# A causal convolution by Fourier transform beside linear attention: a planner's order replaced by tables, with transform pieces of 64 channels

## The chip, the cores and the metric
The kernel runs on one core of a Trainium2 chip. The time is device microseconds of one execution, from launch to end. Five engines work from queues of their own: TensorE (PE, with its weight loads shown as PEld), VectorE (DVE), ScalarE (ACT), GpSimd (POOL) and SyncE (SP), which here issues every DMA. An engine takes its instructions strictly in order, so one that waits holds up all that stand behind it on that engine.

## The reference
Two independent blocks of 2048 positions and 576 channels, bf16, their outputs side by side.

```python
# A: short convolution of k over 4 taps, product with v, long causal convolution by FFT, gate by q
k_shift = sum(k_pad[:, t:t+S, :] * shift_k[:, ks-1-t] for t in range(4))
kv = k_shift * v
y = irfft(rfft(kv padded to 2S) * rfft(ssm_k padded to 2S))[:S] + kv * ssm_D
a = q * y
# B: linear attention with 32 heads of 18 channels
qh, kh, vh = heads of (x @ wqkv);  phi(t) = where(t > 0, t + 1, exp(t)) + 1e-6
o = (phi(qh) @ (phi(kh)' @ vh)) / (phi(qh) . sum(phi(kh)) + 1e-6)
b = o @ wo
out = concatenate([a, b], axis=-1)
```

## The kernel before
**Block A.** The position is split as n = 16a + b, with a on the 128 partitions. Channels go in three chunks (`cc`) of 192. `conv_piece` (L507) does the short convolution on VectorE for one chunk and one half of the sixteen b (`bh`): two tap products of 3072 elements (L518), two sums (L523, L526), a product with v (L529), in place in v. The taps lie in `Wj`, the same row on all partitions: `Wall` is loaded by a DMA that broadcasts 576 KB, and one ScalarE copy of 2304 elements (L493) puts it in order. `h_piece` turns the long filter's rows (`hs`, six pieces of 96 channels) into columns by TensorE transposes.

The transform has two stages. `s1` (L570) multiplies by the tables `Gsb`: for real and imaginary part and for each half of b, eight matmuls of 192 columns into a four-bank PSUM tile, half a bank apart, and one ScalarE copy of 1536 elements (L585) into `Ch` (filter, "h") or `Cu` (signal, "u"). `s2` (L594) takes pieces of `PCH` = 48 channels: a VectorE transpose in 32x32 blocks (L600), 16 small matmuls of 384 columns into a four-bank tile (L612), and two copies of 768 elements by ScalarE or VectorE (L395, L397, the helper `copy`). For the filter, two DMAs (`X`) swap neighbouring partitions into a second tile. `inv` (L632) multiplies the signal's piece by the filter's two tiles (L636, L639), 32 small matmuls (L647) go into a four-bank tile, and two copies put 24 channels each into `V`. There are 12 pieces for h and 12 for u; six pieces make one half of V (288 channels).

`inv2` (L659) ends block A for each half: V goes to a DRAM scratch `v_scr` in rows of 576 bytes, comes back in four loads of `Vt` (rows of 2304 bytes, with the transform index on the partitions), eight matmuls with `Esb` make four positions b (L678), VectorE multiplies by q (L683), and the result is stored.

**Block B.** `kproj` (L693, 16 of them) and `qproj` (L715, 10) project transposed x (`xT`, four groups loaded by transposing DMAs, L445 and L448), ScalarE takes the exponential, VectorE makes phi into `pk` and `pqT`. `b_G` (L755, five) multiplies x by pk, 32 matmuls each; from that come `kvb`, `M` (which holds wo) and the denominators `rden` (a VectorE reciprocal). `b_bc` (L865) spreads rden over the heads' channels in a four-bank tile and VectorE normalizes pqT (L877, ten products of 1024 elements). `b_out` (L883) makes 16 output blocks of 128 positions: ten matmuls of 288 columns (L890), one copy, one store.

**Order.** Each step is an operation of a `Prog` with its engine (or a choice of ScalarE and VectorE), a cost, and what it reads and writes. `Prog.schedule` (L107) issues them in the order of a list schedule: longest remaining path plus a hand-set `BIAS` by group, with `LORDER` for the first loads and limits on live buffers in `LIMIT`. It also places each buffer in SBUF and each tile in PSUM. The order of the result is the order in which instructions go to the engines.

Of the kernel before, what the change touches and what calls it, by code (L numbers as in the profile page):

```python
# [23 lines left out]
PCH = 48  # L24
# [3 lines left out]
class Buf:  # L28
    def __init__(self, name, shape, dt=BF, space="sb", side=0, banks=0, pre=False):
        self.pre = pre  # L30
        self.name, self.shape, self.dt, self.space, self.side, self.banks = name, list(shape), dt, space, side, banks
# [5 lines left out]
        self.left = 0  # L37
        self.pos = None
        self.keys = {}
        self.t = None  # L40
# [6 lines left out]
LAT = 0.12  # L47
SBUF_LO = 16512
SBUF_HI = 229344
DMA_LAT = 2.0  # L50
INF = 1e18


class Prog:
# [9 lines left out]
    def op(self, engs, fn, rd=(), wr=(), name="", bias=0.0, tx=0.0, after=(), use=()):  # L64
# [3 lines left out]
        o.fn, o.name, o.bias, o.tx = fn, name, bias, tx  # L68
# [38 lines left out]
    def schedule(self):  # L107
        ops = self.ops
        n = len(ops)
        succ = [[] for _ in range(n)]  # L110
        nd = [0] * n
        for o in ops:
            for d in o.deps:
                succ[d].append(o.id)
            nd[o.id] = len(o.deps)
        cp = [0.0] * n
        for o in reversed(ops):
            own = min(o.engs.values()) + (o.tx + DMA_LAT if "SP" in o.engs else LAT)
            cp[o.id] = own + max([cp[s] for s in succ[o.id]] + [0.0])
        for o in ops:  # L120
            o.prio = cp[o.id] + (BIAS[o.bias[0]] + o.bias[1] if isinstance(o.bias, tuple) else o.bias)
        engs = ("PE", "ACT", "DVE", "POOL", "SP")
        free = dict.fromkeys(engs, 0.0)
        ready = [0.0] * n
        cand = {e: [] for e in engs}
        for b in self.bufs:
            b.left, b.pos, b.last = b.users, None, 0.0
        for o in ops:
            if nd[o.id] == 0:
                for e in o.engs:  # L130
                    cand[e].append(o)
        bank_free = [0.0] * 8
        live = []
        dma_free = 0.0
        order = []

        def place_ps(b, t):
            best = None
            step = b.banks
            for p in range(0, 8 - b.banks + 1, step):  # L140
                f = max([t] + bank_free[p:p + b.banks])
                if f < INF / 2 and (best is None or f < best[0] - 1e-9):
                    best = (f, p)
            return best

        def place_sb(b, t):
            times = sorted(set([t] + [x[2] for x in live if t < x[2] < INF / 2]))
            lim = LIMIT.get(b.name, 99)
            for tt in times:
                if sum(1 for x in live if x[2] > tt and x[3].name == b.name) >= lim:  # L150
                    continue
                busy = sorted((x[0], x[1]) for x in live if x[2] > tt)
                if b.side == 0:
                    at = SBUF_LO
                    for s, e in busy:
                        if s - at >= b.nbytes:
                            return tt, at
                        at = max(at, e)
                    if SBUF_HI - at >= b.nbytes:
                        return tt, at  # L160
                else:
                    at = SBUF_HI // 32 * 32
                    for s, e in reversed(busy):
                        if at - e >= b.nbytes:
                            return tt, at - b.nbytes
                        at = min(at, s)
                    if at - SBUF_LO >= b.nbytes:
                        return tt, at - b.nbytes
            return None

        def try_place(o, t):
            got = []
            added = []
            ok = True
            saved = None
            for b in o.bufs:
                if b.pos is not None or b.space == "dram":
                    continue
                r = place_ps(b, t) if b.space == "ps" else place_sb(b, t)
                if r is None:  # L180
                    ok = False
                    break
                t = max(t, r[0])
                got.append((b, r[1]))
                if b.space == "sb":
                    added.append([r[1], r[1] + b.nbytes, INF, b])
                    live.append(added[-1])
            for x in added:
                live.remove(x)
            return (t, got) if ok else None  # L190

        for b in self.bufs:
            if b.pre:
                b.pos = place_sb(b, 0.0)[1]
                live.append([b.pos, b.pos + b.nbytes, INF, b])
# [776 lines left out]
```

## Time and profile before

| | before |
|---|---|
| median of 3 runs | 215.75 us (215.52 to 216.03) |
| profiled execution | 215.91 us, span 214.1 us |
| TensorE busy | 164.7 us (77%), 1800 matmuls |
| VectorE busy | 154.9 us (72%), 161 instructions |
| ScalarE busy | 120.8 us (56%), 141 instructions |
| mean granted clock of TensorE | 0.857 of full |
| DMA | 40.09 MB, mean 187 GB/s |

The span runs from the first to the last instruction. Busy time of TensorE counts its pipelined matmuls by modelled ends, so a busy TensorE is not one at its peak. The granted clock is a share of 2.4 GHz.

### The profile page before, as it was taken

How to read it: one execution, taken by the hardware profiler on the slowest of the kernel's cores; microseconds unless marked ns; L12 is line 12 of the kernel's file. 1: busy time of each engine (PE TensorE's matmuls, PEld its weight loads, DVE VectorE, ACT ScalarE, POOL GpSimd, SP SyncE). 2: the span in 40 equal slices, each digit the busy share in tenths (PEclk: the TensorE clock that was granted, in tenths of full speed). 3: DMA queues.
4: the chain of work that ended last, by engine and by line, in shares of the span. 5: the costliest groups of instructions: out<-in, count | busy, mean ns of one | idle time of the engine just before them, and what ended most of it. 6: DMA issues, size and time to landing. Idle time of an engine off the chain costs nothing.

```text
span 214.1 us, 4250 instructions
## 1 busy us (share of the span) xinstructions
PE 164.7 (77%) x1800; PEld 109.6 (51%) x1800; DVE 154.9 (72%) x161; ACT 120.8 (56%) x141; POOL 6.7 (3%) x17
## 2 busy tenths in 40 slices
PE   0660917997898997975899998787577775899993
PEld 0340616655656654751677686255122641576772
DVE  0029999999999899959773073999999799804220
ACT  2071325645989589788846435998986400043442
POOL 7100000000000000100000000000000000000000
PEclk9996785699998799997599999955855895599999
DMA  6899999999340002772790000141199999968543
GB/s 172 199 378 271 362 339 270 215 233 351 97 147 5 2 0 108 237 245 77 300 282 11 0 3 0 53 175 73 41 309 315 298 321 324 354 230 245 187 135 125
DMA packets 39965, 40.09 MB, mean 187 GB/s; under 512 B 11850, under 2 KB 34635, under 8 KB 39178
## 3 DMA queue, kind: packets, MB, share of 16 engines
q1 hardware_dynamic: 39946, 39.82, 61.1%
q8 instruction: 14, 0.23, 0.4%
q14 instruction: 5, 0.04, 0.0%
HBM read 23.04 MB, written 9.44 MB: 152 GB/s over the span
## 4 chain that ended last, share of the span: by engine, by line
PE 40%; DVE 29%; DMA 11%; ACT 10%; issue 7%; SPq 2%; POOL 0%; DVEq 0%; ACTq 0%
PE ps_all L890 10%; PE ps_all L761 9%; DMA Vt<-v_scr 5%; PE ps_all L702 5%; DMA hs<-in_A_ssm_k_dram 5%; DVE m L518 4%; PE ps_all L724 4%; PE ps_all L580 4%; DVE pk L710 3%; DVE ct L600 3%; DVE m L523 3%; ACT Cu L585 3%; PE ps_all L678 2%; DVE sph L636 2%; DVE X L639 2%
## 5 line engine op out<-in xcount | busy, mean ns | idle before, releaser
L702 PE MATMUL ps_all<-wk,xT 128*128 128x288 bf16 x160 | 24.9, 316 | 16.2 <-DMA xT<-in_B_x_dram 14.0
L702 PEld LDWEIGHTS <-xT 128*128 128x128 bf16 x160 | 16.6, 107 | 23.6 <-DMA xT<-in_B_x_dram 14.8
L395 ACT ACTIVATE ob<-ps_all 128x576 bf16<-128x576 f32 x16 | 10.4, 651 | 29.2 <-PE ps_all L890 29.2
L580 PEld LDWEIGHTS <-Gsb 128*128 128x128 bf16 x192 | 20.6, 115 | 8.6 <-issue 5.5
L724 PE MATMUL ps_all<-xT,wq 128*126 128x512 bf16 (+1 forms) x100 | 24.1, 391 | 0.6 <-DVE pqT L731 0.6
L710 DVE SCALAR_TENSOR_TENSOR pk<-ek,ps_all 128x576 bf16<-128x576 bf16 x16 | 11.8, 747 | 16.4 <-ACT ek L707 16.4
L890 PE MATMUL ps_all<-M,pqT 126*128 126x288 bf16 (+1 forms) x160 | 22.0, 299 | 0.5 <-DVE q L683 0.5
L612 PE MATMUL ps_all<-ct,cst 32*32 32x384 bf16 x384 | 15.4, 383 | 8.2 <-DVE ct L600 2.8
L683 DVE TENSOR_TENSOR q<-ps_all,q 128x1152 bf16<-128x1152 f32 x8 | 10.6, 1354 | 15.1 <-PE ps_all L678 15.0
L761 PE MATMUL ps_all<-pk,x_sb 128*128 128x288 bf16 (+1 forms) x160 | 20.6, 286 | 0.6 <-ACT Cu L585 0.4
L518 DVE TENSOR_TENSOR m<-kh,Wj 128x3072 bf16<-128x3072 bf16 x12 | 20.6, 1751 | 0.1
L585 ACT ACTIVATE Ch<-ps_all 128x1536 bf16<-128x1536 f32 x12 | 18.0, 1503 | 2.9 <-PE ps_all L580 2.9
L585 ACT ACTIVATE Cu<-ps_all 128x1536 bf16<-128x1536 f32 x12 | 17.5, 1510 | 3.5 <-PE ps_all L580 3.1
L890 PEld LDWEIGHTS <-pqT 126*128 126x128 bf16 (+1 forms) x160 | 16.3, 102 | 5.9 <-issue 0.7
L707 ACT ACTIVATE ek<-ps_all,neg 128x576 bf16<-128x576 f32 x16 | 11.5, 736 | 13.0 <-PE ps_all L702 11.5
L761 PEld LDWEIGHTS <-x_sb 128*128 128x128 bf16 x160 | 15.5, 98 | 4.8 <-issue 1.0
L724 PEld LDWEIGHTS <-wq 128*126 128x126 bf16 (+1 forms) x100 | 13.2, 137 | 8.7 <-issue 1.9
L580 PE MATMUL ps_all<-v,Gsb 128*128 128x192 bf16 x96 | 14.3, 325 | 2.2 <-ACT Cu L585 1.2
L728 ACT ACTIVATE eq<-ps_all,neg 126x1024 bf16<-126x1024 f32 (+1 forms) x10 | 11.1, 1113 | 7.6 <-PE ps_all L724 7.5
L612 PEld LDWEIGHTS <-cst 32*32 32x32 bf16 x384 | 5.3, 90 | 18.8 <-issue 12.3
L600 DVE STREAM_TRANSPOSE ct<-Ch 128x768 f32<-128x768 f32 x12 | 11.3, 963 | 4.5 <-ACT Ch L585 4.2
L395 ACT ACTIVATE sph<-ps_all 128x768 bf16<-128x768 f32 x18 | 13.8, 824 | 1.0 <-PE ps_all L612 0.9
(63 smaller groups left out, 236.1 us busy)
## 6 DMA issues: line engine op xcount, KB each, us to landing
X<-sph SPq DMA_DIRECT2D x24, 192.0 KB, 2.2
v_scr<-V SPq DMA_DIRECT2D x2, 2304.0 KB, 12.2
Vt<-v_scr SPq DMA_DIRECT2D x8, 576.0 KB, 7.3
v<-in_A_v_dram SPq DMA_DIRECT2D x2, 1152.0 KB, 10.0
hs<-in_A_ssm_k_dram SPq DMA_DIRECT2D x6, 384.0 KB, 11.0
x_sb<-in_B_x_dram SPq DMA_DIRECT2D x1, 2304.0 KB, 10.9
q<-in_A_q_dram SPq DMA_DIRECT2D x2, 1152.0 KB, 6.6
out_dram<-q SPq DMA_DIRECT2D x8, 288.0 KB, 4.8
```

The costliest lines, as they stand in the source:

```text
L395: nc.scalar.activation(out=o, in_=i, func=ACTF.Copy)
L518: nc.vector.tensor_tensor(out=m.t[:, i:i + 2], in0=i0, in1=i1, op=ALU.mult)
L580: nc.tensor.matmul(ps.t[:, j // 2, 256 * (j % 2):256 * (j % 2) + CC], lhsT=Gsb.t[:, b, ri, :], rhs=src, start=True, stop=True)
L585: nc.scalar.activation(out=C.t[:, :, rb:rb + 8, :].rearrange("p w r t -> p r w t"), in_=ps.t.rearrange("p b (h c) -> p (b h) c", h=2)[:, : ...
L600: nc.vector.transpose(out=ct.t[:].rearrange("p w r t -> p (w r t)").bitcast(FP32), in_=C.t[:, nw * pi:nw * pi + nw].rearrange("p w r t -> ...
L612: nc.tensor.matmul(o, lhsT=W2()[32 * kh:32 * kh + 32, :], rhs=ctf[32 * kh:32 * kh + 32, 384 * j:384 * j + 384], start=True, stop=True)
L702: nc.tensor.matmul(ps.t[:, hh, 0:HALF], lhsT=xT.t[:, t, 128 * rr:128 * rr + 128], rhs=wk.t[:, t, HALF * hh:HALF * hh + HALF], start=(t == ...
L707: P.op(("ACT", _act(576) + 0.09), lambda e: nc.scalar.activation(out=eb.t[:], in_=ps.t[:, :, 0:HALF], func=ACTF.Exp, bias=neg1.t[:]), rd=[ ...
L710: P.op(("DVE", _dve(576)), lambda e: nc.vector.scalar_tensor_tensor(out=pk.t[:, r, 0:D].rearrange("p (h c) -> p h c", h=2), in0=eb.t[:], s ...
L724: nc.tensor.matmul(ps.t[0:hn, j, :], lhsT=wq.t[:, t, h0:h0 + hn], rhs=xT.t[:, t, :], start=(t == 0), stop=(t == 4))
L761: nc.tensor.matmul(ps.t[:, hh, 0:n], lhsT=x_sb.t[:, r, FT[t]:FT[t] + 128], rhs=pk.t[:, r, HALF * hh:HALF * hh + n], start=(r == 0), stop=( ...
L890: nc.tensor.matmul(ps.t[:, hh, 0:HALF], lhsT=pqT.t[0:hn, c, 128 * r:128 * r + 128], rhs=M.t[0:hn, c, HALF * hh:HALF * hh + HALF], start=(c ...
```

## The change
The planner is gone. Two tables stand in its place: `PLAN`, one word for each of the 573 operations in issue order with its engine, and `PLACES`, the place of each buffer. With it:

- `PCH` is 64, so there are 9 pieces for h and 9 for u. A piece's second stage and its inverse each run as two steps in two-bank PSUM tiles, with matmuls of 512 columns and copies of 1024 elements. The products with the filter are of 2048 elements, and the `X` swaps are issued in the signal's part.
- The first stage packs its eight blocks of 192 columns without gaps into three banks; a block that straddles a bank is two matmuls. Its copy may be on either engine.
- V's halves are 320 and 256 channels (five and four pieces). V is written to DRAM in one run per partition; it is read back in 32 loads of 32 partitions (every fourth one), in rows of 640 or 512 bytes. The last stage works in two-bank tiles: eight steps of two positions for the first half, four of four for the second.
- The taps come as one row of 4.6 KB; matmuls of a row of ones with it spread the row over the partitions, and two ScalarE copies of 1152 elements make `Wj`.
- The first 192 columns of `kh0` and of its three earlier rows are loaded apart from the rest.
- The normalization runs in ten steps of two banks, so the second half's positions can go first.

In the table, the queue of TensorE begins with the filter's transposes and its first stage, then the first k blocks; the five G blocks stand together with the last filter pieces and the first chunk of u; seven normalizations, M and output blocks 9, 13 and 14 stand ahead of the last piece of V; ten output blocks stand between it and the first i2 step of V's second half. SP's queue begins with cst, hs, khh, Drow, hs, srow, Gsb, kh0 (192 columns), khh, then xT 0, wk, xT 1, v0, kh1, wq, v1, three hs, the rest of kh0, and the transposed loads of groups 2 and 3.

```diff
-PCH = 48
+PCH = 64
+VN = (320, 256)
+VP = (0, 5)
...
-    order = P.schedule()
+    order = _issue(P)
...
+def _issue(P):
+    names = dict(P="PE", A="ACT", D="DVE", G="POOL", S="SP")
+    order = []
+    for w in PLAN.split():
+        o = P.ops[int(w[1:])]
+        o.eng = names[w[0]]
+        order.append(o)
+    places = [int(w) for w in PLACES.split()]
+    for b, p in zip([b for b in P.bufs if b.space != "dram"], places, strict=True):
+        b.pos = p
+    return order
...
-    load("Wall", Wall, lambda e: dma(Wall.t[:].rearrange("p d j -> p (d j)"),
-                                     A_shift_k.rearrange("d j -> (d j)").partition_broadcast(128)), 589824,
+    load("srow", srow, lambda e: dma(srow.t[:], A_shift_k.rearrange("(o d) j -> o d j", o=1)), 4608,
+    for hh in range(2):
+        wps = psb(4, "wps")
+        def wmm(e, hh=hh, wps=wps):
+            for j in range(4):
+                nc.tensor.matmul(wps.t[:, j, 0:HALF], lhsT=ones.t[0:1, :],
+                                 rhs=srow.t[0:1, HALF * hh:HALF * hh + HALF, j], start=True, stop=True)
...
-                ps = psb(4, "s1ps")
+                ps = psb(3, "s1ps")
...
+                        for bank, lo, hi in banks(CC * j, CC * j + CC):
+                            nc.tensor.matmul(ps.t[:, bank, lo - 512 * bank:hi - 512 * bank], lhsT=Gsb.t[:, b, ri, :],
+                                             rhs=src[:, lo - CC * j:hi - CC * j], start=True, stop=True)
...
+        for kp in range(2):
+            ps = psb(2, "s2ps")
+            def mm(e, kp=kp, ps=ps):
+                for j in range(4):
+                    for kk in range(2):
+                        kh = 2 * kp + kk
+                        nc.tensor.matmul(
+                            ps.t[32 * j:32 * j + 32, kk, :].rearrange("p (k w t) -> p w k t", w=8, t=2),
+                            lhsT=W2()[32 * kh:32 * kh + 32, :], rhs=ct.t[32 * kh:32 * kh + 32, 8 * j:8 * j + 8],
+                            start=True, stop=True)
...
+            P.op(either(1024), lambda e, kp=kp, ps=ps: copy(e, sp.t[:, 2 * kp:2 * kp + 2, :], ps.t),
...
-        w_ = load("Vw", None, lambda e: dma(ap(vd, 0, [[HALF, 128], [128 * HALF, 32], [1, HALF]]), V[hf].t[:]),
+        load("Vw", None, lambda e: dma(vd, V[hf].t[:].rearrange("p k c -> p (k c)")), 8192 * n, rd=[V[hf]], wr=[dtok],
...
+                vt = SB("Vt", [128, 8, n])
+                for kh in range(4):
+                    load("Vr", vt, lambda e, b4=bg * nb, vt=vt, kh=kh: dma(
+                        vt.t[kh:128:4], ap(vd, (32 * kh + 2 * b4) * 32 * n, [[n, 32], [32 * n, 8], [1, n]])),
```

## Rows read from the trace of the kernel before

**Rows 1.** Busy time by stretch: from:to us, length, busy us (count) of each engine, clock, DMA share, GB/s.
```profile
0.00:14.90 14.90, 6.77 (x40) 4.34 (x40) 0.01 (x1) 4.32 (x4) 4.56 (x13) 1.00 0.83 237
14.90:92.30 77.40, 60.06 (x482) 42.04 (x483) 76.22 (x77) 49.46 (x52) 2.12 (x4) 0.87 0.66 196
92.30:139.30 47.00, 39.24 (x585) 26.97 (x585) 28.05 (x32) 31.38 (x41) 0.00 (x0) 0.93 0.29 100
139.30:166.80 27.50, 20.72 (x423) 10.03 (x423) 26.52 (x31) 23.23 (x29) 0.00 (x0) 0.58 0.61 186
166.80:185.50 18.70, 13.18 (x85) 7.56 (x84) 17.51 (x19) 1.96 (x3) 0.00 (x0) 0.77 1.09 319
185.50:214.10 28.60, 24.71 (x189) 18.69 (x187) 6.63 (x6) 10.42 (x16) 0.00 (x0) 0.96 0.61 197
sum 214.10, PE 164.68 PEld 109.63 DVE 154.94 ACT 120.76 POOL 6.68; mean PE 27.45 PEld 18.27 DVE 25.82 ACT 20.13 POOL 1.11
```

**Rows 2.** Chain of waits, in order of time: start us, us, what.
```profile
107.14 4.11 PE ps_all L761 x32
...
171.55 11.08 DMA Vt<-v_scr
...
210.76 0.65 ACT ob L395
```

**Rows 3.** Groups of VectorE instructions: total us, mean ns of one, idle before.
```profile
L636 DVE TENSOR_TENSOR sph<-spu,sph 128x1536 bf16<-128x1536 bf16 x12 | 11.3, 944 | 0.0
L600 DVE STREAM_TRANSPOSE ct<-Ch 128x768 f32<-128x768 f32 x12 | 11.3, 963 | 4.5 <-ACT Ch L585 4.2 <-PE ps_all L612 0.2
L683 DVE TENSOR_TENSOR q<-ps_all,q 128x1152 bf16<-128x1152 f32 x8 | 10.6, 1354 | 15.1 <-PE ps_all L678 15.0
L877 DVE SCALAR_TENSOR_TENSOR pqT<-pqT,ps_all 126x1024 bf16<-126x1024 bf16 x8 | 9.3, 1212 | 0.0
L397 DVE CAST V<-ps_all 128x768 bf16<-128x768 f32 x8 | 7.4, 951 | 0.6 <-PE ps_all L647 0.5
L397 DVE CAST spu<-ps_all 128x768 bf16<-128x768 f32 x7 | 6.5, 937 | 1.6 <-PE ps_all L612 1.6
L397 DVE CAST sph<-ps_all 128x768 bf16<-128x768 f32 x6 | 5.4, 935 | 0.0
L397 DVE CAST M<-ps_all 126x576 bf16<-126x576 f32 x1 | 0.7, 746 | 0.0
```

**Rows 4.** Groups of ScalarE copies from PSUM.
```profile
L585 ACT ACTIVATE Cu<-ps_all 128x1536 bf16<-128x1536 f32 x12 | 17.5, 1510 | 3.5 <-PE ps_all L580 3.1 <-DVE sph L397 0.5
L395 ACT ACTIVATE spu<-ps_all 128x768 bf16<-128x768 f32 x17 | 13.3, 823 | 0.9 <-PE ps_all L612 0.9
```

**Rows 5.** SP's queue at the start, in order of time: start us, us, instruction.
```profile
9.09 9.36 SPq L445 DMA_TRANSPOSE xT<-in_B_x_dram  x1
...
23.25 12.81 SPq L445 DMA_TRANSPOSE xT<-in_B_x_dram  x1
```

**Rows 6.** Busy time in three stretches; the last column is DMA in GB/s.
```profile
0.00:30.00 30.00, 13.36 (x80) 8.61 (x80) 15.00 (x13) 9.06 (x10) 5.07 (x14) 0.89 0.92 290
158.00:163.80 5.80, 4.11 (x98) 1.19 (x98) 5.80 (x7) 5.13 (x8) 0.00 (x0) 0.50 1.13 302
171.50:177.30 5.80, 4.15 (x33) 2.52 (x31) 5.71 (x6) 0.30 (x1) 0.00 (x0) 1.00 1.13 316
```

**Rows 7.** SP's queue from the first write of V on.
```profile
153.61 0.40 SPq L382 DMA_DIRECT2D v_scr<-V  x1
...
163.87 1.87 SPq L382 DMA_DIRECT2D Vt<-v_scr  x3
167.01 0.38 SPq L382 DMA_DIRECT2D v_scr<-V  x1
...
181.31 4.01 SPq L382 DMA_DIRECT2D Vt<-v_scr  x3
```

**Rows 8.** Output blocks on TensorE, in order of time.
```profile
193.75 5.09 PE L890 MATMUL ps_all<-M,pqT 126*128 126x288 bf16 x40 [0.47 <-DVE q L683]
```

More of the change, by code (lines that the diff above doesn't have):

```diff
@@ L269 @@
-WIN = 0.05
+def _issue(P):
[8 more added lines that the diff above has]
+        b.pos = p
+    assert sorted(o.id for o in order) == list(range(len(P.ops)))
+    return order
 def _tables():
@@ L331, in _tables, with banks @@
     return G.astype(bf), E.astype(bf), C.astype(bf)
+def banks(lo, hi):
+    got = []
+    while lo < hi:
+        e = min(hi, lo // 512 * 512 + 512)
+        got.append((lo // 512, lo, e))
+        lo = e
+    return got
 def _pe(*ns):
@@ L338, in _act, with _dma @@
 def _act(n):
-    return 0.19 + n * 0.000833
+    return 0.17 + n * 0.000868
 def _dve(n, rate=1):
-    return 0.065 + n * 0.00104 / rate
-def _dma(nb):
-    return nb / 330000.0
+    return 0.145 + n * 0.001045 / rate
+def _dma(nb, row=4096):
+    return nb / (16.0 * row / (8.0 + row * 0.0412) * 1000.0)
 @with_exitstack
@@ L462, in f2 @@
             dma(wx.t[64:128, 4, :], wqkv[512:576, c0:c0 + D])
-        load("wqk" + key, wx, f1, 589824, wr=[(wx, "m")])
+        load("wqk" + key, wx, f1, 589824, wr=[(wx, "m")], row=1152)
         load("wqkt" + key, wx, f2, 73728, wr=[(wx, "t")])
@@ new lines, in s2 @@
+        for kp in range(2):
[8 more added lines that the diff above has]
+                            start=True, stop=True)
+            aft = [seq[x] for x in (nm, ("h", g)) if x in seq] if kp == 0 else []
+            last = P.op(("PE", T8), mm, rd=[ct, cst], wr=[ps], use=[sp], name="s2" + nm, bias=bias, cnt=8, after=aft)
+            P.op(either(1024), lambda e, kp=kp, ps=ps: copy(e, sp.t[:, 2 * kp:2 * kp + 2, :], ps.t),
+                 rd=[ps], wr=[(sp, kp)], name="s2ev" + nm, bias=bias)
@@ new lines, in s2 @@
+        seq[nm] = last
+        seq[(nm, g)] = last
+        if nm == "h":
+            TX[g] = sp
+        return g, sp
+    V = [SB("V%d" % i, [128, 32, VN[i]], side=1) for i in range(2)]
+    def inv(g, su, bias):
+        tx = TX[g]
+        hf = int(g >= VP[1])
+        c0 = PCH * (g - VP[hf])
+        xb = SB("X", [128, 4, 512])
+        load("X", xb, lambda e: dma(xb.t[0:128:2], tx.t[1:128:2]), 262144, rd=[tx], wr=[(xb, 0)], bias=bias, row=4096)
+        load("X", xb, lambda e: dma(xb.t[1:128:2], tx.t[0:128:2]), 262144, rd=[tx], wr=[(xb, 1)], bias=bias, row=4096)
+        P.op(("DVE", _dve(2048, 2)),
@@ new lines, in inv, with mm, ev @@
+        for jp in range(2):
+            ps = psb(2, "i1ps")
+            def mm(e, jp=jp, ps=ps):
+                for wi, (w, src) in enumerate(((W31, tx), (W32, xb))):
+                    for kh in range(4):
+                        for jj in range(2):
+                            j = 2 * jp + jj
+                            nc.tensor.matmul(ps.t[32 * kh:32 * kh + 32, jj, :],
+                                             lhsT=w()[32 * j:32 * j + 32, :],
+                                             rhs=src.t[32 * j:32 * j + 32, kh, :],
+                                             start=(wi == 0), stop=(wi == 1))
+            P.op(("PE", 2 * T8), mm, rd=[tx, xb, cst], wr=[ps], use=[V[hf]], name="i1", bias=bias, cnt=16)
+            def ev(e, jp=jp, ps=ps):
+                o0 = c0 + 32 * jp
+                copy(e, V[hf].t[:, :, o0:o0 + 32].rearrange("p k (j c) -> p j k c", c=16),
+                     ps.t.rearrange("p j (k c) -> p j k c", c=16))
+            P.op(either(1024), ev, rd=[ps], wr=[(V[hf], (g, jp))], name="i1ev", bias=bias)
```

470 lines of the change are left out of this document (144 added, 326 removed), and 12 rows, old and new, of the table PLACES.

## The prediction
> **What bounds the kernel now.** I read the busy time by stretch first [rows 1]. VectorE is the fullest engine with 154.9 of 214.1 us, and its idle time has three places. In the first 14.9 us it does nothing. From 14.9 to 92.3 us it is busy 76.2 of 77.4 us, so there its own work is the limit. From 92.3 to 139.3 us it is busy for only 28.05 of 47 us; there the chain of waits runs through TensorE blocks of 32 matmuls of 4.11 us each (the product x'·pk, five of them) and through what queues behind them [rows 2]. From 139.3 to 166.8 us, the stage of products and inverse transforms, VectorE is full again, 26.52 of 27.5 us. At 166.8 us the last piece of V has left PSUM. What follows takes 47.3 us, more than a fifth of the time, and holds no transform of the first stages at all: V goes to DRAM and comes back, VectorE normalizes all of pqT (17.5 of 18.7 us busy), the chain waits 11.08 us for Vt [rows 2], and only then TensorE starts the 16 output blocks, which fill the last 28.6 us (24.7 us of TensorE beside 6.6 us of VectorE). In this tail work that does not depend on V stands in a row with work that does. So the time is: VectorE's sum, plus its gaps at the start and in the middle, plus a tail in which it is mostly free.
>
> **What the edits do to VectorE's sum.** The pieces of 64 move the same elements in fewer, longer instructions. A PSUM copy costs 0.94 us for 768 elements and a PSUM product 1.354 us for 1152 [rows 3], so about 1.08 ns an element; 1024 elements would be 1.21 us (an estimate from those two rows).
> - PSUM copies of the transforms: before 8+7+6 on VectorE, 19.3 us [rows 3]; the table puts 4+4 there, 8 x 1.21 = 9.7 us: -9.6.
> - Transposes: 24 x 0.96 = 22.2 us become 18 of 1024, 18 x (0.963 + 256 x 0.00108) = 22.3: 0.
> - The products with spu: 24 x 0.947 = 22.7 us become 18 of 2048 elements. At the same fixed part (half speed per element, 0.53 ns) 18 x 1.21 = 21.9: -0.8.
> - Last products with q: 8 x 1.354 = 10.6 us become 8 x 0.80 + 4 x 1.22 = 11.3: +0.7.
> - Moved to VectorE by the table: one stage-1 copy of 1536 (1.77 us), six output copies (6 x 0.75), two GT copies and one gcol (1.7), two hT copies (at most 2 x 0.75, nearest row, I take 1.1); moved off it: two M copies (-1.4). Together +7.7.
> Sum -2.0: 152.9 us. ScalarE evicts one 1536-block less and four pieces' worth more; by 1.51 and 0.82 us [rows 4] it stays within 3 us of its 120.8. TensorE has the same columns. The packed stage-1 tile adds two matmuls to each eight because blocks of 192 straddle banks; 48 more issues, hidden under the copies (1.51 us against the eight matmuls). If not hidden, the bound is 48 x 0.13 us (a 288-column matmul of the output takes 5.09/40 [rows 8]) = 6 us, and below nothing it can save: three banks instead of four let two tiles stand beside a two-bank one. I take 0. The row copies of the taps swap a broadcast of 576 KB and one copy of 2304 elements for 4.6 KB, eight matmuls and two copies of 1152: ScalarE the same, DMA 0.59 MB less, about 2 us at 290 GB/s [rows 6], which the start uses.
>
> **The start.** The table has SP issue cst, two hs, Gsb, the first 192 columns of kh0 and the tiny tap row ahead of the first transposed x. So VectorE has hT copies and the first taps well before 14.9 us. But then it needs v0 and kh1, which stand behind two transposed x. What must have landed before the second time block's taps is 7.4 MB; the first 30 us moved 290 GB/s, 8.7 MB [rows 6], so kh1 lands at 26 to 31 us. By then the table gives VectorE 16.2 us of work (5 hT copies and additions, 4 taps and sums, 3 transposes, 6 kphi, one product with v). Idle there: 31 - 16 = 15 us, as much as before. I book no gain here; bounds 10 to 20.
> Next SP comes to the last four transposed loads with some 6.6 MB outstanding. Before, such an issue stood 9.36 and 12.81 us [rows 5] while 4 to 5 MB drained. All that must land ahead of the last x is 13.3 MB (before: 12.3, without four of the hs), so it lands at about 53 us; TensorE's queue has the first q block of the second half there, with stage 1 of h and all later k blocks behind it, and VectorE reaches its qphi at 31 + 22 = 53 us but can have it at 53 + 3.4 (q block, exp): 4 us idle. Bounds 0 and 12.
> At this place the rows of kh0 become 384 and 768 bytes long instead of 9 KB. The nearest rows are 576-byte transfers (V and q): 302 GB/s [rows 6], against 316 with 2304-byte rows; by that 0.39 MB costs 1.3 us, and if a 384-byte packet takes as long as a 576-byte one 2.0 us. I take 0 more on the path, because Gsb lands beside it; bound 1.
> The Trainium skill (DMA: Bandwidth & Descriptors, Specifications) says that transfers under 512 bytes fall below line rate because they are read, modified and written. No row here shows that rate for a plain load; were it half, the estimate by that page would be 1.3 us more at the first taps, inside the bounds.
>
> **The middle.** Counted from the table, the five G blocks stand close together, with stage 1 and 2 of u between them. VectorE's u transposes wait for two stage-1 blocks behind the first G (about 1.5 us), its next copy for two G blocks of 4.11 us (2), then the GT copies for G block 3 (3) and the first product (1.5): 8 us idle, against 19 before. Bounds 4 and 19. The stage of products was 96% full before [rows 1]; two-bank tiles let the next half start while the first is copied, but each copy is on ScalarE, which also is nearly full (33 beside 34.6 us of VectorE in the table). I take 3 us idle; bounds 1 and 8.
> So the last V copy starts at VectorE work 134.3 (152.9 less 18.6 that the table leaves behind it: 3 normalizations of 1.18, 12 q products, 5 output copies) plus 15 + 4 + 8 + 3 = 30 idle: 164.3 us. Before it was 166.8 with 130.3 us of work done. The gain is not here: 7 of 10 normalizations, 3 output blocks and all of M are now ahead of this point.
>
> **The tail.** After 164.3: last copy 1.0; V's second half is now 2.1 MB instead of 2.36 (256 columns); the first write of before took from 153.61 to 163.87 [rows 7], 10.3 us, so 9.2, plus 0.3 issue. The read back is 16 loads: issue 0.62 each (1.87 for three [rows 7]) is 9.9 us, above the 6.6 us of bytes at 316 GB/s, then 2.7 to land; six output stores between them, 0.4 each, some 1.6 on the path: 14.2. Then the last i2 block and its product, 1.1 + 1.2, store issue 0.4 and 2.7 until the span ends (as before from 211.4 to 214.1 [rows 2]). Sum 1.0 + 9.5 + 14.2 + 2.3 + 3.1 = 30.1 us. TensorE has 13 output blocks of 5.09/4 = 1.27 us [rows 8], i2 and three bc: about 25 us, VectorE 18.6; both fit. Bytes agree: from the first V write, 18 us before this point, 15 MB are left, 48 us at 316 GB/s, which ends 30 us after it. Bounds: 25 (TensorE's sum) and 38 (write 14.3 as the second one took, from 167.0 to 181.3 [rows 7], and 3 us of SP waits).
> On that queue the Trainium skill (DMA: Bandwidth & Descriptors, Queues, rings and completion order) says that descriptors of one engine are consumed in ring order. The second V write, issued with Vt reads ahead of it, took 14.3 us against 10.3, which agrees; by that rule the write would cost 4 us more here too, if the first half's reads still run.
>
> Span 164.3 + 30.1 = 194.4. The profiled execution took 215.9 with a span of 214.1, so 1.8 outside; the median of runs is 0.2 lower. Predicted 194.4 + 1.8 - 0.2 = 196.
>
> **Rivals.**
> 1. The order holds better: the middle idles 4, the start 12, tail 26: 152.9 - 18.6 + 12 + 0 + 4 + 2 + 26 = 178.3, so 180. For it: VectorE ran 98% full for 77 us. Against: the G blocks are 4 us each and nothing can pass them in a fixed queue. Chance 0.12.
> 2. The start gives half the gain back: the last x lands 8 us later, middle as 12 instead of 8: 208. For it: SP stood 12.81 us at one such load. Against: 0.59 MB less to move. Chance 0.20.
> 3. Slower: the read back is priced by the load, not by bytes. A Vt load before was 256 packets for 0.59 MB, 1.87 us at 316 GB/s; now 32 loads of 256 packets each. At 1.87 us each the 16 of the second half take 29.9 instead of 9.9: +20 us, and the first half's push the second write back by some 4: 220. It decides from 1.8 us a load. Against it: 4096 packets of 576 bytes went at 302 GB/s. Chance 0.10.
> 4. The tail keeps its 47.3 us: the output blocks ahead of V's return wait for the last normalizations, which stand behind VectorE's copies, and run after i2 as before. Then 164.3 + 1.0 + 47.3 + 1.6 = 214.2, and with the start 1.5 us later, inside its bounds, 215.7: no change. Against: the table issues 3 of 16 before the last V copy and 10 ahead of the second half's i2. Chance 0.03.
> The forecast itself (188 to 203) has 0.55.
>
> **How the numbers follow.** The range takes all of the forecast and most of rivals 1 and 2: 182 to 211. A measurement tells 0.2% from no change. Faster: 0.55 + 0.12 + 0.20 = 0.87; same 0.03; slower 0.10.
>
> **What would show it.** Right: VectorE near 153 us; the first taps before 14 us but the second block's not before 26; a hole of some 4 us at the q block of the second half; VectorE's idle time in the G blocks under 12 us; last V copy near 164; from there 30 us with TensorE at work on output blocks while V is written. Wrong: 32 Vt loads that take over 1 us each; TensorE waiting over 10 us for xT; V's last copy after 175 us.

## The result and the profile after

The changed kernel takes 198.56 us (median of 4 runs, 196.38 to 199.05) against 215.63 for the kernel before, run beside it: ratio 0.92, 95% interval 0.9118 to 0.9282. Some executions of one kernel are over 1.5% longer than its fastest; the ratios leave them out, the medians and ranges do not. The forecast was 196 with a range of 182 to 211. The profiled execution took 199.05 us with a span of 197.3, so 1.75 lie outside the span, as before.

Busy time by stretch of the changed kernel (columns as in [rows 1]). The cuts: first taps, taps of the second time block, start and end of the G blocks, end of the last copy of V, first read of V's second half, end of the last product.
```profile
0.00:11.00 11.00, 5.69 (x49) 4.53 (x50) 2.07 (x5) 3.37 (x4) 4.04 (x12) 1.00 0.88 265
11.00:29.70 18.70, 15.36 (x107) 10.71 (x106) 14.60 (x14) 11.33 (x12) 1.03 (x2) 0.82 0.97 282
29.70:91.90 62.20, 55.84 (x486) 39.28 (x484) 60.19 (x57) 45.95 (x47) 1.79 (x4) 0.95 0.54 154
91.90:108.20 16.30, 15.75 (x172) 11.69 (x170) 11.12 (x12) 7.91 (x11) 0.00 (x0) 1.00 0.59 213
108.20:161.40 53.20, 46.38 (x676) 24.59 (x674) 47.27 (x45) 46.30 (x50) 0.00 (x0) 0.78 0.54 168
161.40:171.99 10.59, 10.18 (x80) 7.20 (x79) 6.62 (x7) 3.14 (x5) 0.00 (x0) 1.00 0.96 348
171.99:190.20 18.21, 13.66 (x109) 10.23 (x107) 11.49 (x13) 1.95 (x3) 0.00 (x0) 1.00 0.73 221
190.20:197.30 7.10, 0.00 (x0) 0.00 (x0) 0.00 (x0) 0.00 (x0) 0.00 (x0) 0.73 0.77 221
sum 197.30, PE 162.85 PEld 108.23 DVE 153.35 ACT 119.95 POOL 6.85; mean PE 20.36 PEld 13.53 DVE 19.17 ACT 14.99 POOL 0.86
```
VectorE's work is nearly what it was (153.35 against 154.94 us), but it stands elsewhere. Up to the last copy of V it now does 135.25 us of work in 161.4 us, 26.15 idle; before it was 130.8 in 166.8, 36.0 idle [rows 1]. The hole in the middle has shrunk most: 5.2 us are idle in the 16.3 us of the G blocks, where it was 18.95 in 47. The two cuts do not hold the same work; from the G blocks to the last copy of V together it is 11.1 us idle in 69.5, and was 19.9 in 74.5. In the stretch ahead of them VectorE idles 1.0 us less than before. After the last copy of V the kernel before needed 47.3 us; this one needs 35.9. So of 16.8 us of span, 5.4 are won up to that copy and 11.4 behind it.

SP's queue in the tail of the changed kernel (it answers to [rows 7]):
```profile
161.53 1.27 SPq L240 DMA_DIRECT2D Vt<-v_scr  x2
162.91 0.53 SPq L240 DMA_DIRECT2D v_scr<-V  x1
...
171.99 9.13 SPq L240 DMA_DIRECT2D Vt<-v_scr  x14
...
181.80 2.45 SPq L240 DMA_DIRECT2D Vt<-v_scr  x2
...
190.58 2.13 SPq L240 DMA_DIRECT2D out_dram<-q  x3
192.76 0.86 SPq L240 DMA_DIRECT2D out_dram<-ob  x1
```
Three things are to be seen here. V is complete at 161.4, but its write is issued at 162.91, behind reads of the first half. Fourteen reads take 9.13 us of issue, 0.65 each; 128 KB in 0.65 us is 201 GB/s, so up to the first late step the return goes at the pace of SP. And the last store is issued 3.4 us after the last product (190.18). The chain of waits walks along that queue, one issue after the other, to the first late step of the inverse on TensorE (it answers to [rows 2]):
```profile
177.88 0.61 SPq L240
178.49 0.04 issue
178.53 2.58 DMA Vt<-v_scr
181.11 0.14 issue
181.25 1.03 PE ps_all L550 x8
```
Behind that step VectorE waits once for an output block's store, whose buffer it needs:
```profile
185.30 0.76 DVE L250 CAST ob<-ps_all 128x576 bf16<-128x576 f32 x1 [1.03 <-DMA out_dram<-ob]
```
Some of VectorE's groups, answering to [rows 3]; the pieces of 64 make them fewer and longer:
```profile
L500 DVE TENSOR_TENSOR X<-spu,X 128x2048 bf16<-128x2048 bf16 x9 | 10.8, 1213 | 0.0
L503 DVE TENSOR_TENSOR sph<-spu,sph 128x2048 bf16<-128x2048 bf16 x9 | 10.8, 1215 | 0.4 <-ACT spu L248 0.4
L463 DVE STREAM_TRANSPOSE ct<-Cu 128x1024 f32<-128x1024 f32 x9 | 10.7, 1218 | 0.3 <-ACT Cu L248 0.3
L250 DVE CAST V<-ps_all 128x1024 bf16<-128x1024 f32 x4 | 4.8, 1209 | 1.5 <-PE ps_all L513 1.5
```

### The profile page after: what moved, and what is told of

Read it like the earlier page. It is cut to its first block, busy times and chain, and to the rows that moved or that the text cites. A ratio compares the mean times of both kernels' runs of the same rounds, so it can differ in the third digit from the quotient of the medians.

```text
span 197.3 us, 3955 instructions
## 1 busy us (share of the span) xinstructions
PE 162.8 (83%) x1664; PEld 108.2 (55%) x1664; DVE 153.4 (78%) x150; ACT 120.0 (61%) x127; POOL 6.9 (3%) x18
## 4 chain that ended last, share of the span: by engine, by line
PE 37%; DVE 24%; ACT 12%; SPq 11%; issue 7%; DMA 6%; DVEq 1%; ACTq 0%
PE ps_all L636 8%; SPq L240 7%; PE ps_all L599 6%; PE ps_all L577 6%; PE ps_all L766 6%; DVE m L383 5%; PE ps_all L445 5%; DMA Vt<-v_scr 3%; ACT Cu L248 3%; DVE X L500 3%; SPq L299 2%; DVE pk L585 2%; DVE ct L463 2%; DMA wk<-in_B_wqkv_dram 2%; PE ps_all L550 2%
## 5 line engine op out<-in xcount | busy, mean ns | idle before, releaser
L577 PE MATMUL ps_all<-wk,xT 128*128 128x288 bf16 x160 | 23.4, 306 | 2.5 <-DMA wk<-in_B_wqkv_dram 2.5
L766 PE MATMUL ps_all<-M,pqT 126*128 126x288 bf16 (+1 forms) x160 | 23.5, 305 | 0.2 <-ACT V L248 0.2
L248 ACT ACTIVATE sph<-ps_all 128x1024 bf16<-128x1024 f32 x16 | 16.2, 1028 | 4.4 <-PE ps_all L476 4.4
L248 ACT ACTIVATE spu<-ps_all 128x1024 bf16<-128x1024 f32 x16 | 15.9, 1028 | 4.7 <-PE ps_all L476 4.7
L248 ACT ACTIVATE Ch<-ps_all 128x1536 bf16<-128x1536 f32 x11 | 16.1, 1523 | 2.5 <-PE ps_all L445 2.3
L248 ACT ACTIVATE ob<-ps_all 128x576 bf16<-128x576 f32 x10 | 6.5, 652 | 17.7 <-PE ps_all L766 17.3
L445 PE MATMUL ps_all<-hT,Gsb 128*128 128x192 bf16 (+2 forms) x120 | 12.8, 272 | 5.3 <-DVE hT L425 3.4
L476 PE MATMUL ps_all<-ct,cst 32*32 32x512 bf16 x288 | 13.2, 438 | 4.0 <-ACT Cu L248 0.9
L603 ACT ACTIVATE eq<-ps_all,neg 126x1024 bf16<-126x1024 f32 (+1 forms) x10 | 11.1, 1114 | 7.8 <-PE ps_all L599 7.8
L248 ACT ACTIVATE V<-ps_all 128x1024 bf16<-128x1024 f32 x14 | 13.7, 1035 | 2.7 <-PE ps_all L513 2.7
L555 DVE TENSOR_TENSOR q<-ps_all,q 128x640 bf16<-128x640 f32 (+1 forms) x12 | 11.0, 953 | 5.5 <-PE ps_all L550 4.6
## 6 DMA issues: line engine op xcount, KB each, us to landing
v<-in_A_v_dram SPq DMA_DIRECT2D x2, 1152.0 KB, 11.1
```

The costliest lines, as they stand in the source:

```text
L248: nc.scalar.activation(out=o, in_=i, func=ACTF.Copy)
L445: nc.tensor.matmul(ps.t[:, bank, lo - 512 * bank:hi - 512 * bank], lhsT=Gsb.t[:, b, ri, :], rhs=src[:, lo - CC * j:hi - CC * j], start=Tru ...
L476: nc.tensor.matmul(ps.t[32 * j:32 * j + 32, kk, :].rearrange("p (k w t) -> p w k t", w=8, t=2), lhsT=W2()[32 * kh:32 * kh + 32, :], rhs=ct ...
L577: nc.tensor.matmul(ps.t[:, hh, 0:HALF], lhsT=xT.t[:, t, 128 * (r % 4):128 * (r % 4) + 128], rhs=wk.t[:, t, HALF * hh:HALF * hh + HALF], st ...
L603: P.op(("ACT", _act(1024) + 0.09), lambda e: nc.scalar.activation(out=eb.t[0:hn], in_=ps.t[0:hn], func=ACTF.Exp, bias=neg1.t[0:hn, :]), rd ...
L766: nc.tensor.matmul(ps.t[:, hh, 0:HALF], lhsT=pqT.t[0:hn, c, 128 * r:128 * r + 128], rhs=M.t[0:hn, c, HALF * hh:HALF * hh + HALF], start=(c ...
```

## The experiments

In the tables `P238 A239 S240` are the matmuls, the copy and the store of one output block; a pair such as `P205 D206` is one normalization step. An i2 step is one step of `inv2`: the matmuls that make some positions of V's half, and the product with q. All times are medians, ratios are to the kernel before as it ran beside that run; there its median lay between 214.62 and 216.17, so two runs are told apart by their ratios first. The change's own ratio is 0.9118 to 0.9282. A trace is one execution: that of the change is its longest (199.05 us), those of V's way and of the two queues are the shortest of theirs, so a difference of 1 or 2 us between traces can be one of executions.

**Is it the order of the tail?** First all sixteen output blocks were put behind the last i2 step of V's first half, as they stood in the kernel before.
```diff
-A468 P456 S517 D499 P238 S527 A457 S536 S526 D500 P250 S534 A489 D474 P501 A239 P253 ...
+A468 P456 S517 D499 S527 A457 S536 S526 D500 S534 A489 D474 P501 ...
...
+P238 A239 P250 A251 P253 A254 P235 A236 ...
```


> The changed kernel with one thing undone: all 16 output blocks stand behind the first half's last i2 step, four ahead of each later i2 step, as the kernel before had them; pieces, normalizations and everything else stay. Theory A (the tail got shorter because output blocks run while V is written and read): 13 blocks now fill that wait; put behind it, i2 of the first half ends at about 171 us, four blocks at 176, the second half's Vt comes at 181 as now, and 12 blocks of 1.25 us and four i2 steps follow, 18 us, then 4 to the end: 203 to 205 us, 5 to 6 more than the 198.6 of the change. Theory B (the gain is in the pieces of 64 and two-bank steps, the place of the output blocks does not matter): within 1 us of 198.6.

Measured: 207.77 (206.81 to 209.67), ratio 0.9657 (0.9608 to 0.9706): +9.2 us. TensorE after the last V copy:
```profile
165.27 3.28 PE L550 MATMUL ps_all<-Vt,Esb 128*128 128x320 bf16 x12 [3.83 <-DMA Vt<-v_scr]
...
177.10 1.39 PE L766 MATMUL ps_all<-M,pqT 126*128 126x288 bf16 x10 [0.79 <-ACT ob L248]
...
184.48 5.10 PE L766 MATMUL ps_all<-M,pqT 126*128 126x288 bf16 x40
189.42 1.04 PE L550 MATMUL ps_all<-Vt,Esb 128*128 128x256 bf16 x8
```
TensorE waits for V's first half, then for ScalarE (0.8 us a block), and twelve blocks stand in the last 23 us, each later i2 step behind four of them. Theory A holds, with a price above its range of 5 to 6 us. Part of that is not the place of the blocks: the edit also puts all sixteen copies on ScalarE, where six were on VectorE. And TensorE, which had waited 3.83 us for V, does its first i2 steps at a granted clock of 0.53, the lower of its two levels (1.2 and 2.4 GHz):
```profile
165.27:168.55 3.28, 3.27 (x12) 1.72 (x13) 0.82 (x1) 0.00 (x0) 0.00 (x0) 0.53 1.04 445
```
In the change, with output blocks in that wait, the same 12 matmuls took 1.79 us at a clock of 1.00.

Then, on top of this, the seven early normalizations went behind the last V copy.
```diff
-... P195 P420 A421 D196 P433 ... P407 D408 A465 P462 D440 P193 A463 P458 D194 ...
+... P420 A421 P433 ... P407 D408 A465 P462 D440 A463 P458 ...
...
+... P201 D202 P203 D204 P205 D206 P207 D208 P209 D210 P193 D194 P195 D196 ...
```


> As the run with the output blocks behind, and the seven normalizations that the change put ahead of V's last copy stand behind it too. Theory A': VectorE is the engine that sets V's last copy, so 7 x 1.13 = 7.9 us less ahead of it bring that copy from 161 to 153 to 156 us, and the normalizations then run while V is written: 2 to 5 us less than with the output blocks alone, about 200 us. Rival: the normalizations filled VectorE's gaps ahead of V's last copy, so the copy moves by under 2 us, the tail has 8 us more VectorE work before the first output block, and it takes 3 to 8 us more, 207 to 212.

Measured: 213.2 (211.75 to 214.0), ratio 0.9881 (0.983 to 0.9932): +5.4 on the run before. The row that decides is VectorE's:
```profile
157.61 1.23 DVE L250 CAST V<-ps_all 128x1024 bf16<-128x1024 f32 x1 [1.94 <-ACT V L248]
159.07 11.39 DVE L753 SCALAR_TENSOR_TENSOR pqT<-pqT,ps_all 126x1024 bf16<-126x1024 bf16 x10 [0.23 <-PE ps_all L747]
```
With seven steps of 1.2 us less in front of it, the last copy of V ended at 160.4, 1.2 us earlier than in the run before. The normalizations had stood in gaps of VectorE and had cost V next to nothing; behind it the 11.39 us of all ten (three stood there before) hold up the q products. The rival holds (5.4 lies inside its 3 to 8 us), and A' falls. Both moves together undo 14.6 of the 17 us.

**Could the old shapes take that order?** The kernel before, its order written out, with normalizations, kv and M ahead of the last V copy and output blocks beside V's write (bc and pqn are the normalization, out an output block, Gev the copy of a G block, s1ev, s2ev and i1ev copies of the transforms out of PSUM).
```diff
-    order = P.schedule()
+    order = _issue(P)
...
```
The moves in its table, in words: bc.0-4 and pqn behind s1evh.7, s2evu.11, i1ev.3, s2evh.11, s2evh.15; kv behind Gev.3; M among s1evu.8-11; out.0-3 behind V's second write, out.4-7 behind the second i2 product, out.8-15 behind the fourth to the seventh.

> The kernel before (pieces of 48, four-bank steps, V's rows, taps by broadcast, its planner's order written out), with only the last steps moved: the ten normalizations, kv and M stand ahead of V's last copy, and the output blocks beside V's write and reads. Theory A (order of the tail is the gain): V's last copy comes some 5 us later, the tail falls from 47 to about 33: 206 to 209 us. Theory B (pieces and two-bank steps are the gain): 214 to 217.

Measured: 235.03 (234.3 to 237.63), ratio 1.0933 (1.0874 to 1.0992), outside both theories. TensorE in its stage of products:
```profile
136.55 0.34 PE L466 MATMUL ps_all<-ct,cst 32*32 32x384 bf16 x2 [1.38 <-DVE pqT L731]
137.69 0.38 PE L466 MATMUL ps_all<-ct,cst 32*32 32x384 bf16 x14 [0.80 <-DVE pqT L731]
...
141.99 0.43 PE L725 MATMUL ps_all<-rden,cst 32*126 32x512 bf16 x2 [0.83 <-DVE spu L251]
...
148.12 0.50 PE L501 MATMUL ps_all<-sph,cst 32*32 32x384 bf16 x2 [1.19 <-DVE pqT L731]
```
A normalization tile of four banks and a transform tile of four banks take all eight banks that the kernel has, so the transform's matmuls (L466, L501) wait for VectorE to read the normalization's tile, and the normalization's (L725) for the transform's reader. The last V copy ended at 189.5, and the tail behind it, 46.4 us, is hardly shorter than before: in it SP, whose queue holds the reads of V too, waited 18.1 us for the copies of output blocks. So this run says only that four-bank tiles do not take this interleaving, not what the order is worth. It was tried again, with normalizations in two-bank tiles and only five of them moved, beside the last G blocks. The moves in its table, in words: bc.5-7 and pqn.5-7 ahead of G.3; bc.8-9 and pqn.8-9 behind Gev.3; out.8-11 behind the third i2 product, out.12-15 behind pqn.4, out.0-7 behind the fourth to the eighth i2 product.

> The kernel before with its planner's order written out and three things moved or cut: the normalization runs in two-bank tiles, its five steps for the second 1024 positions stand beside the last two G blocks, where VectorE idled, and output blocks 8 to 15 stand between the first half's third and fourth i2 step, where TensorE waited for Vt. Pieces of 48, four-bank steps, V's rows and the taps stay. Theory A (order of the tail is the gain): 10 us of output blocks and 5.7 us of normalizations leave the tail: 204 to 207 us. Theory B (pieces and two-bank steps are the gain): 214 to 217.

Measured: 217.31 (216.53 to 217.97), ratio 1.0113 (1.0066 to 1.016). TensorE around the moved steps:
```profile
130.24 0.43 PE L726 MATMUL ps_all<-rden,cst 32*126 32x512 bf16 x2 [0.88 <-DVE pqT L732]
132.50 5.77 PE L615 MATMUL ps_all<-pk,x_sb 128*128 128x288 bf16 x32 [1.83 <-DVE pqT L732]
```
and its busy time from there on, cut at the end of the last copy of V:
```profile
139.30:175.40 36.10, 24.95 (x588) 11.03 (x588) 35.47 (x40) 29.28 (x36) 0.00 (x0) 0.65 0.49 147
175.40:215.80 40.40, 33.40 (x262) 25.05 (x260) 18.72 (x18) 12.24 (x19) 0.00 (x0) 0.96 0.94 290
```
The tail fell from 47.3 to 40.4 us, but the last V copy moved from 166.8 to 175.4: the last G block now waits for VectorE, and VectorE is 98% full from 139.3 on. So 6.9 us are won in the tail and 8.6 lost ahead of it. A falls: in this order the moved work displaces V. The time lies just above B's range, but that does not show B, since nothing in this run has the new shapes of the transform.

**Do the shapes do it alone?** All the new shapes and loads under the planner of before, with its priorities, and buffer limits wide enough for the new tiles.
```diff
-    order = _issue(P)
+    order = P.schedule()
...
+LIMIT = dict(ct=6, spu=6, ek=3, eq=3, ob=4, hs=2, Cu=2, Ch=2, Vt=3, sph=8, X=8, hT0=1)
```


> All the new shapes (pieces of 64, two-bank steps, packed PSUM, V's new rows, taps by outer product), but the order by the planner of before with its priorities, load list and an SBUF limit loosened so that it finds places, in place of the tables. Theory A (the tables' order is the gain): 211 to 218. Theory B (the shapes are the gain): 198 to 204.

Measured: 239.33 (237.45 to 240.74), ratio 1.1134 (1.105 to 1.1218). SP's queue at the start:
```profile
10.84 7.95 SPq L459 DMA_TRANSPOSE xT<-in_B_x_dram  x1
...
23.41 14.12 SPq L459 DMA_TRANSPOSE xT<-in_B_x_dram  x1
```
It is outside both theories. That the shapes do it alone falls. It shows that they need an order of their own, but the size does not measure the tables' order: the planner's priorities had been set for the old pieces, cst and Gsb come behind two transposed loads here, and VectorE was given 168.6 us of work.

**V's way through DRAM** as before: rows written, four reads of 128 partitions for each half.
```diff
-dma(vd, V[hf].t[:].rearrange("p k c -> p (k c)"))
+dma(ap(vd, 0, [[n, 128], [128 * n, 32], [1, n]]), V[hf].t[:])
...
-                vt = SB("Vt", [128, 8, n])
-                for kh in range(4):
+                vt = SB("Vt", [128, 2, 4, n])
```


> The changed kernel with V's way through DRAM as before: written in rows of 640 and 512 bytes (4096 a half), read back in four loads a half of 128 partitions with rows of 2560 and 2048 bytes. Theory C (32 short loads in single file cost the tail SP's issue time): 16 issues of 0.61 us become 4, the second half's last row lands up to 5 us sooner: 194 to 196. Theory D (bytes and the wait for the write set it; the two layouts trade a quick write for a quick read): 198 to 200. Rival E (short rows make the write slow, as the 14.3 us of the second write before suggests): 202 to 204.

Measured: 196.4 (195.36 to 196.79), ratio 0.9134 (0.9091 to 0.9177): 2.2 us faster than the change by the medians, 1.4 by the ratios, whose intervals overlap; just above C's range. Rival E falls. SP's queue, and behind it the busy time of the stretch from the first read on, here and in the change:
```profile
161.75 0.38 SPq L240 DMA_DIRECT2D v_scr<-V  x1
162.29 5.58 SPq L240 DMA_DIRECT2D out_dram<-ob  x1
...
171.72 2.65 SPq L240 DMA_DIRECT2D Vt<-v_scr  x4
```
```profile
171.70:179.50 7.80, 7.45 (x59) 5.38 (x57) 4.86 (x7) 1.30 (x2) 0.00 (x0) 1.00 0.96 273
```
```profile
171.99:181.10 9.11, 7.38 (x57) 5.29 (x55) 5.29 (x7) 1.30 (x2) 0.00 (x0) 1.00 0.68 198
```
The write costs 1 us more here (10.0 from its issue to the first read against 9.1), the return 2.5 us less: 15.7 from the first read to the last product (187.4) against 18.2. SP's issue that follows the write in short rows stands 5.58 us (a store of 144 KB; behind the change's write four of them took 4.59 us together), so the short rows hold SP at the write and the short reads hold it at the return. Four issues leave SP free, and the bytes move at 273 GB/s instead of 198 in the first 9 us of the return. The edit changes the number of reads and the length of their rows (2048 bytes instead of 512) together. Alone this run does not settle that this part of the change is a loss; a pair of runs below agrees in the direction.

**The taps** by the broadcast load of before.
```diff
-    load("srow", srow, lambda e: dma(srow.t[:], A_shift_k.rearrange("(o d) j -> o d j", o=1)), 4608,
+    load("Wall", Wall, lambda e: dma(Wall.t[:].rearrange("p d j -> p (d j)"),
+                                     A_shift_k.rearrange("d j -> (d j)").partition_broadcast(128)), 589824,
```


> The changed kernel with the taps loaded as before: 576 KB broadcast by DMA in the place of the 4.6 KB row, one ScalarE copy of 2304 elements, no outer product. Theory F (the start is set by bytes ahead of kh and v): 0.59 MB at 290 GB/s, the first taps at 13 instead of 11 us, the second block's at 31.7 instead of 29.7, end 2 us later: 200 to 201. Rival (hidden, since VectorE waits 13 us in the start anyway): within 0.5 us of 198.6.

Measured: 202.61 (201.53 to 203.51), ratio 0.9436 (0.9375 to 0.9497): +4.0 by the medians, 5.1 by the ratios. VectorE:
```profile
14.59 3.43 DVE L374 TENSOR_TENSOR m<-kh,Wj 128x3072 bf16<-128x3072 bf16 x2 [4.39 <-DMA kh<-in_A_k_dram]
...
32.63 3.43 DVE L374 TENSOR_TENSOR m<-kh,Wj 128x3072 bf16<-128x3072 bf16 x2 [1.12 <-DMA kh<-in_A_k_dram]
...
46.05 3.43 DVE L374 TENSOR_TENSOR m<-kh,Wj 128x3072 bf16<-128x3072 bf16 x2 [1.72 <-DMA kh<-in_A_k_dram]
```
and the same place in the changed kernel:
```profile
11.01 3.43 DVE L383 TENSOR_TENSOR m<-kh,Wj 128x3072 bf16<-128x3072 bf16 x2 [1.87 <-DMA kh<-in_A_k_dram]
...
29.73 3.42 DVE L383 TENSOR_TENSOR m<-kh,Wj 128x3072 bf16<-128x3072 bf16 x2
```
The 0.59 MB stand in the queue ahead of kh, whose longest issue there stands 4.42 us (1.69 in the change): the first taps come 3.6 us later, the second block's 2.9, and the third's wait once more. F holds in kind, but its 2 us were too small, and the rival falls.

**What is left in the tail?** Half of the sixteen late reads on ScalarE's queue:
```diff
+                        hf == 1 and kh % 2 == 1),
```


> The changed kernel, with 8 of the 16 reads of V's second half issued by ScalarE's DMA queue. Theory C (SP's issue in single file, 0.61 us each, sets the tail): the reads are out in 5 us instead of 10, so the last i2 step starts some 4 us earlier and the end comes 3 to 4 us earlier: 194.5 to 195.5. Rival (the bytes set it, 2.1 MB at some 316 GB/s beside the stores): at most 1 us less, 197.5 to 198.6.

Measured: 198.74 (196.18 to 200.13), ratio 0.914 (0.9091 to 0.9188): no difference from the change that can be told, so theory C falls as far as the runs can tell. SP's and ScalarE's queues:
```profile
172.10 5.93 SPq L240 DMA_DIRECT2D Vt<-v_scr  x7
```
```profile
173.23 5.99 ACTq L240 DMA_DIRECT2D Vt<-v_scr  x6
```
An issue that took 0.65 us alone takes 0.85 and 1.0 with two queues at work. Together they are somewhat quicker: the stretch from 172.1 to 179.2 moves 241 GB/s with rows of 512 bytes, so the 198 above are not set by the rows alone. From SP's first read to the first late i2 step it is 8.55 us instead of 9.26. In this execution the last product, too, comes sooner (16.5 us after SP's first read, 18.2 in the change), but it is the shortest of six that end between 196.18 and 200.13, and the runs as a whole do not show it. Then the stores of the second half's products on ScalarE's queue:
```diff
-                    qb.t[:, b4:b4 + 4, :]), 1024 * n,
+                    qb.t[:, b4:b4 + 4, :], hf == 1), 1024 * n,
```


> The changed kernel, with only this moved: the four stores of the second half's products are issued on ScalarE's DMA queue instead of SP's. In the changed kernel the last product ends at 190.18 and SP issues three product stores at 190.58 (2.13 us) and an output block at 192.76 (0.86), the end is 197.3. Theory Q (the last 4 us of the tail are SP's queue: one store after another, half a microsecond each): with the product stores on another queue SP's last store is issued before 189 and ScalarE's at about 190.8, landing 2.5 to 3.7 us later, so the span ends at 193.5 to 195 and the median falls by 2.5 to 4 us, to 194.5 to 196. Rival L (the stores end when their bytes are through, 7.1 us after the last product whatever the queue): within 1 us of the changed kernel's 198.6. Rival S (a DMA issue costs ScalarE more than SP and delays its last output copy): slower by up to 1 us.

Measured: 201.13 (199.05 to 203.4), ratio 0.9318 (0.9251 to 0.9386). SP's queue, and behind it the busy time from the last product (192.9) on:
```profile
191.86 1.04 SPq L240 DMA_DIRECT2D out_dram<-q  x1
192.99 2.55 SPq L240 DMA_DIRECT2D out_dram<-ob  x2
```
```profile
192.90:199.20 6.30, 0.00 (x0) 0.00 (x0) 0.00 (x0) 0.00 (x0) 0.00 (x0) 0.60 0.78 235
```
From the last product to the end it is 6.3 us instead of 7.1; SP's stores took 1.3 us each beside ScalarE's. Theory Q falls: the end shrinks by 0.8 us only, near what L says, though the whole misses L's range. S does not explain that, since ScalarE's last copy (186.20) stands ahead of its stores. The whole ran 2.6 us longer by the medians, but the ratios' intervals overlap, so it is not settled that it is slower at all; in its trace V was complete 0.6 us later, and the first half's reads, which the edit does not touch, landed 2.9 us later. The same with V's way of before:

> Both improvements together: V's way through DRAM as in the kernel before (four reads of a half, 196.4 us alone) and the four stores of the second half's products on ScalarE's DMA queue. Theory Q: as SP in that kernel issues its last store at 187.84 already, half a microsecond after the last product, little of the queue is left to take away: 194.5 to 196.4. Rival L (bytes): 196.4 within 0.6. If the two gains added up fully it would be 192.5 to 194.

Measured: 196.94 (193.47 to 198.6), ratio 0.9058 (0.8968 to 0.9148): no gain over V's way alone that can be told. Between these two kernels, which ran side by side, V's way is worth 4.2 us by the medians, and the intervals do not overlap (0.8968 to 0.9148 against 0.9251 to 0.9386). So with the stores on ScalarE's queue the change's way is a loss, and the run above points the same way. The Trainium skill (DMA: Bandwidth & Descriptors, Issuing engines are not separate DMA queues) says that transfers from different engines' queues end up on the same sixteen DMA engines. The two-queue runs do not contradict it: an issue got longer (0.65 to 0.85 and 1.0 us), and no time was gained that can be told. It adds that what a second queue saves in issue is usually small beside the transfer. Here it is not small: a read of 128 KB took 0.65 us of issue, and at the 273 GB/s of the four larger reads its bytes would take 0.48 us (an estimate from those two rows).

Last, the bytes: each output block's store cut from 128 rows to 16, the other rows left unwritten.
```diff
-dma(outd[128 * r:128 * r + 128, D:2 * D], ob.t[:])
+dma(outd[128 * r:128 * r + 16, D:2 * D], ob.t[0:16])
```


> The changed kernel with only this altered: each of the sixteen stores of attention's output blocks moves 16 of its 128 rows (18 KB in place of 144 KB; the other rows of that half of the output are left unwritten). The number of issues, their order and all the computing stay. Thirteen of the sixteen are issued between 163 and 193.6, so 1.6 MB of some 8 MB that the tail moves go. Theory B (the tail's transfers share the DMA engines, and the bytes of the blocks' stores lengthen V's write, its return and the last stores): 1.6 MB at the 250 GB/s of that stretch is 6.5 us of the engines; first late products some 2 to 3 us earlier than 181.25, the end within 5 us of the last product in place of 7.1, and the median 3 to 6 us lower: 192.5 to 195.5. Rival Q (issues and fixed latencies set the tail, the stores fit beside): within 1 us of 198.6.

Measured: 196.21 (195.56 to 198.64), ratio 0.9058 (0.9037 to 0.908): 2.4 us less by the medians, 3.1 by the ratios, for 1.6 MB. That is at or just above B's range, and the rival falls. Its profiled execution was its longest, 2.4 us above the median, so its lines do not show where the gain is; in it V was complete at 163.2 and the end came 33.6 us later (35.9 in the change), with 6.5 after the last product:
```profile
164.37 0.53 SPq L240 DMA_DIRECT2D v_scr<-V  x1
...
172.97 9.14 SPq L240 DMA_DIRECT2D Vt<-v_scr  x14
```
The write is 0.5 us shorter and the issue of the reads not at all. So the bytes of the blocks are worth some 3 us of the tail. What sets the rest is not settled: the reads' issue bounds the way to the first late step in the trace, yet halving it on a second queue gave nothing that can be told.

## Why the prediction was right, and where its terms were off

The direction and the mechanism (tail work beside V's trip) were right, and the size came out close: 197.3 of span against 194.4. That closeness is in part luck, for it is the sum of two errors of opposite sign: V was complete at 161.4 instead of 165.3 (the forecast's start 164.3 and its 1.0 us of copy), 3.9 us early, and what follows took 35.9 instead of 29.1, 6.8 us more.

- *VectorE's sum* (152.9): 153.35. The estimate of 1.21 us for 1024 elements out of PSUM was 1.209 to 1.224; 18 products 21.6 (21.9), 18 transposes 21.4 (22.3), q products 11.1 (11.3). One reading was off: the work ahead of the last V copy of the kernel before is 130.8 us by [rows 1], not 130.3; the forecast does not rest on it.
- *Start* (15 us idle): 13.0, and the second block's taps at 29.73, inside 26 to 31. But the taps' row copies were booked as nothing on the path, and undoing them costs 4 to 5 us. "About 2 us", which "the start uses", was too small, and it then had no place in the sum: the 0.59 MB stand ahead of the very loads that VectorE waits for, three times.
- *Late x* (4): VectorE waited 1.34 us at 53.18 for the q block, at the place forecast. In the whole stretch it idled 2.0.
- *G blocks* (8, bounds 4 to 19): 5.2. *Products* (3, bounds 1 to 8): 5.9.
- *"The gain is not here"*: this step failed, for a third of the gain is there (5.4 of 16.8 us). The idle time of VectorE ahead of the last V copy fell by 9.9 us, though seven normalizations more stand ahead of it; they fill gaps (the second run).
- *Tail*: the write (9.5 with issue) took 9.1, but was issued 1.5 late behind reads, as the upper bound had it. The reads, priced at 0.62 an issue, took 0.65. From the first read to the last product 16.5 were booked and 18.2 measured: the last three i2 steps and their products run in one row behind two output blocks, one of whose copies waited 1.03 us for a store. The term that was mis-sized is the last, 3.1 from the last product to the end: 7.1. It was taken from before, where a single output block was left; here three product stores and a block are, SP's last issue ends 3.4 us after the last product, and 4 us are missing. A second queue took 0.8 of it.
- *Second write.* The Trainium skill (DMA: Bandwidth & Descriptors, Queues, rings and completion order) says that each DMA engine takes its descriptors in ring order. From that the prediction drew 4 us more for the second write, if the first half's reads still ran. Their last two were issued at 161.53, just ahead of the write, and it took 9.1 us for 2.1 MB; the first write, 2.6 MB with no reads ahead of it but a load of q beside it, took 10.1. A delay of 4 us does not show.
- *Rivals.* The load-priced read back needed over 1.8 us an issue; the median of 32 was 0.61. The unshortened tail and the late start did not come, and neither did the better order (180).

What each part is worth, as far as the runs go: the place of the output blocks about 9 us (with six copies on the other engine) and of the normalizations 5 (together 14.6), the taps 4 to 5, V's way through DRAM a loss of 1 to 2, not clear of the noise by itself; they overlap and do not add to the 17. What the shapes are worth without an order of their own was not isolated: the old shapes did not take the new order in two attempts, and the new shapes were tried only under priorities made for the old.

## What to carry to other kernels

At a round trip through DRAM, look which independent work stands behind it, and put it ahead only where the engine it needs has gaps; in the one old-shape order where that engine was full, the move lost 8.6 us to win 6.9. Of bytes taken out of a queue, ask which load stood behind them and who waits for that one. Price the end by all the stores that are still to be issued after the last result, not by the landing of one.

## What the runs showed of the hardware

An issue on SP is not a constant: 0.65 us for a 128 KB read with one queue, 0.85 and 1.0 with SP and ScalarE issuing at once. A 144 KB store took 0.55 us (the change, at 181.22), 1.15 behind V's write (four from 163.54), 1.3 beside four product stores on ScalarE's queue, and 5.58 right behind V's write in rows of 512 bytes. The return of V's second half moved 198 GB/s with reads of 128 KB on one queue, 241 with them on two, and 273 with four reads of 512 KB, other stores included. And one edit at the end of the queue (the stores on ScalarE) went with a first half that landed 2.9 us later, which nothing here explains.
